# Emitting the first batch's routing at the head of the next quad in a fused attention, top-1 MoE and FFN kernel

## The chip, the core and the metric

The kernel runs on one core of a Trainium2 chip. The metric is the device time of one launch in microseconds. Of the engines, PE (TensorE) does all matmuls and the transposes through the identity, DVE (VectorE) and ACT (ScalarE) empty its PSUM banks and prepare operands, POOL (GpSimd) does elementwise work in SBUF, and SP (SyncE) issues most DMAs. Each engine takes its instructions strictly in the order of the built program, so an instruction that waits holds up all that stand behind it on its engine.

## What is computed

```
q_p, k_p = phi(q_s), phi(k_s)            # random features, exp(h - max) per row; 4 batches, 8 heads, 576 tokens
kv = einsum('bhsm,bhsd->bhmd', k_p, v); z = k_p.sum(2)
attn = einsum('bhsm,bhmd->bhsd', q_p, kv) / (einsum('bhsm,bhm->bhs', q_p, z)[..., None] + 1e-6)
x = attn.transpose(0, 2, 1, 3).reshape(2304, 512)
logits = x @ w_gate                      # 8 experts, each token goes to its argmax
out[mask] = gate_w[mask, None] * (relu(x[mask] @ w1[e]) @ w2[e])
h = out @ w_in; g = h * sigmoid(1.702 * h); y = g @ w_out
```

## The kernel before

The attention works on **quads** of four heads, two quads to a batch, eight in all. For quad `i`, `kgen(i)` projects the keys (`ph_P`, PSUM tile `pr`) and sums `kv_ps`; `qgen(i)` runs 17 steps on the queries in the order `Q_ORDER`: `P` projects (`pr`, L350 and L351), `X` transposes (`tq`, L430), `N` forms the normalised output (`num`, L444), `R` transposes it for the MoE (`tx`, `small`, L464 and L466). Each `P` takes a row maximum and a subtraction on DVE (L359, L368, L380). `halves_T` splits the next quads' inputs into two f16 halves (ACT L307, POOL L308, squares on POOL L267 and L272) and sends them through a transposing DMA on SP (`xT`, L309, three buffers).

When both quads of a batch are done, `route(b)` finds the expert that most of the batch's tokens chose: logits on PE (`lT_ps`, L529 and L530), transposes (`lg_ps`, L537), a chain of small DVE operations (L542 to L554, `oh` is the one-hot), a count over all partitions on PE (`ct_ps`, L561), and its argmax on DVE (`es`, L571). SP loads `es` into a register (L604), and with it issues the loads of that expert's weights (`st`, L674, eight chunks of 512 KB for a batch). ACT and POOL (DVE for the first chunk and for the last batch) split each chunk into `wh` and `wl` (L698, L700). `moe_gen(b)` then multiplies in three passes (L136; PSUM tiles `m_ps` and `w_ps`), 384 matmuls of 128x288 for a batch, with `h1h` on ACT (L732) and `h1l` on DVE (L735) between its two layers. Tokens that chose another expert than their batch's are counted and would be done by a general loop behind it.

The order of the program has three sources. The generators of attention are merged by weight: `merge` always advances the generator that has the smallest share of steps done over weight. The main loop runs attention alone until the first batch's gate stands (`while 0 not in gate_t`), then alternates attention and MoE by accumulated cost, counted from the point at which MoE began. And a scheduler reorders instructions by priority when the program is built. `route` has seven steps; the weights are 17 for `qgen`, `ROUTE_N` = 10 for `route` and 5 for `kgen`. From tick 245 of the loop on, jobs for the FFN's weights (`prep_outs`, `z` tiles on DVE, `raw_o` loads and `wo_dram` stores issued by ACT) are mixed in. The FFN follows when the MoE is done.

## Time and profile before

| | us |
|---|---|
| median of 3 runs | 768.23 (766.17 to 768.77) |
| the profiled execution: time | 767.65 |
| its span, first to last instruction | 765.6 |
| PE busy in the span | 739.7 (97%) |
| DVE, ACT, POOL busy | 531.3, 338.6, 131.9 |
| mean granted TensorE clock | 0.99 of full speed |

PE is busy nearly all of the span, so a microsecond is lost or won where PE waits or runs at a lower clock. The share of the span says little by itself; the stretches in which PE is not full are few, and they are what to read.

### The profile page before, as it was taken

What the parts mean: (1) busy time and instruction counts of PE and PEld (TensorE: products, weight loads), DVE (VectorE), ACT (ScalarE), POOL (GpSimd) and SP (SyncE); (2) the same over time, 40 slices, a digit from 0 to 9 for tenths busy, and PEclk for the clock granted to TensorE, in tenths of its full rate; (3) what the DMA queues carried; (4) which work ended last, traced back from release to release, by engine and by line L of the source; (5) the groups of instructions that cost most, each with busy time, mean ns of one, the idle gap of its engine ahead of it and who ended that gap; (6) DMA issues with size and microseconds to landing.
All of it is one profiled execution on the core that took longest, in us unless ns stands there. A gap on an engine that the chain in (4) does not pass through costs nothing.

```text
span 765.6 us, 14359 instructions
## 1 busy us (share of the span) xinstructions
PE 739.7 (97%) x5559; PEld 716.1 (94%) x5559; DVE 531.3 (69%) x1188; ACT 338.6 (44%) x638; POOL 131.9 (17%) x78
## 2 busy tenths in 40 slices
PE   7998799999999999989999999999999999999997
PEld 6877699999999999979999999999999999999996
DVE  5867867586776685556879559981368777777774
ACT  5554464335522332233427464554576433444331
POOL 3563377609500441000000000000000000000000
PEclk9999799999999999999999999999999999999999
DMA  5447594456725554198145558972978544443311
GB/s 157 117 131 187 123 302 97 120 140 193 189 60 162 150 179 134 51 234 287 59 161 197 177 171 295 316 263 100 332 273 298 172 138 138 137 129 117 115 29 32
DMA packets 136715, 127.57 MB, mean 167 GB/s; under 512 B 58176, under 2 KB 120896, under 8 KB 135744
## 3 DMA queue, kind: packets, MB, share of 16 engines
q1 hardware_dynamic: 123936, 98.85, 43.5%
q10 hardware_dynamic: 12704, 27.73, 10.3%
q8 instruction: 45, 0.74, 0.4%
q14 instruction: 30, 0.25, 0.1%
HBM read 79.68 MB, written 40.40 MB: 157 GB/s over the span
## 4 chain that ended last, share of the span: by engine, by line
PE 83%; DVE 8%; DMA 4%; issue 1%; ACT 1%; SPq 1%; POOL 0%; ACTq 0%; POOLq 0%; DVEq 0%
PE m_ps L136 19%; PE qa L1249 13%; PE qa L1146 13%; PE qm L1249 7%; PE w_ps L136 4%; PE pb L1249 3%; PE qm L1146 3%; PE qu L1146 3%; PE num L444 3%; PE kv_ps L402 3%; DMA st<-in_moe_w_dram 2%; PE qn L1146 2%; PE qt L1146 2%; PE tq L430 1%; PE pr L344 1%
## 5 line engine op out<-in xcount | busy, mean ns | idle before, releaser
L1146 PE MATMUL qa<-y,wi 128*128 128x384 f32 x576 | 109.2, 337 | 0.4 <-DVE g L901 0.4
L1146 PEld LDWEIGHTS qa<-y,wi 128*128 128x128 f32 x576 | 101.4, 188 | 0.8 <-DVE g L901 0.8
L136 PE MATMUL m_ps<-xh,wh 128*128 128x288 f32 x256 | 79.0, 309 | 4.1 <-DVE h1l L735 2.3
L136 PE MATMUL m_ps<-xh,wl 128*128 128x288 f32 x256 | 76.8, 300 | 0.1
L136 PE MATMUL m_ps<-xl,wh 128*128 128x288 f32 x256 | 76.4, 298 | 0.0
L700 POOL TENSOR_TENSOR wl<-st,wh 128x1024 fp32r<-128x1024 f32 x23 | 55.1, 2401 | 83.0 <-ACT wh L698 82.9
L359 DVE TENSOR_REDUCE small<-pr 128x4 f32<-128x512 f32 (+1 forms) x80 | 51.1, 639 | 11.8 <-PE pr L351 7.8
L698 ACT ACTIVATE wh<-st 128x1024 fp32r<-128x1024 f32 (+1 forms) x33 | 34.0, 1035 | 48.5 <-DMA st<-in_moe_w_dram 31.6
L136 PEld LDWEIGHTS m_ps<-xh,wh 128*128 128x128 f32 x256 | 48.6, 190 | 5.8 <-DVE h1l L735 3.6
L136 PE MATMUL m_ps<-h1h,wh 128*128 128x288 f32 x160 | 48.8, 305 | 0.9 <-DVE h1l L735 0.9
L136 PEld LDWEIGHTS m_ps<-xh,wl 128*128 128x128 f32 x256 | 48.6, 190 | 0.5 <-DVE wl L700 0.4
L735 DVE SCALAR_TENSOR_TENSOR h1l<-m_ps,h1h 128x288 fp32r<-128x288 f32 x64 | 28.9, 453 | 28.9 <-ACT h1h L732 28.8
L136 PEld LDWEIGHTS m_ps<-xl,wh 128*128 128x128 f32 x256 | 48.6, 190 | 0.0
L136 PE MATMUL m_ps<-h1l,wh 128*128 128x288 f32 x160 | 47.7, 298 | 0.0
L136 PE MATMUL m_ps<-h1h,wl 128*128 128x288 f32 x160 | 47.4, 298 | 0.0
L732 ACT ACTIVATE h1h<-m_ps 128x288 fp32r<-128x288 f32 x64 | 25.9, 407 | 48.5 <-PE m_ps L136 46.7
L1249 PE MATMUL qa<-p,p 128*128 128x256 f32 x360 | 46.2, 282 | 1.1 <-DVE p L855 0.8
L1249 PE MATMUL qa<-p,gs 128*128 128x256 f32 x360 | 45.9, 282 | 0.0
L1249 PEld LDWEIGHTS qa<-p,p 128*128 128x128 f32 x360 | 44.2, 189 | 1.6 <-DVE p L855 1.0
L1249 PEld LDWEIGHTS qa<-p,gs 128*128 128x128 f32 x360 | 44.2, 189 | 0.0
L444 PEld LDWEIGHTS num<-kv,qpT 128*128 128x128 f32 (+1 forms) x320 | 36.7, 184 | 5.4 <-ACT qpT L432 3.1
L444 PE MATMUL num<-kv,qpT 128*128 128x65 f32 (+1 forms) x320 | 39.3, 266 | 2.5 <-ACT qpT L432 1.4
(213 smaller groups left out, 1819.5 us busy)
## 6 DMA issues: line engine op xcount, KB each, us to landing
g_dram<-g ACTq DMA_DIRECT2D x48, 384.0 KB, 4.1
st<-in_moe_w_dram SPq DMA_DIRECT2D x31, 512.0 KB, 5.2
pg<-g_dram SPq DMA_DIRECT2D x10, 1024.0 KB, 5.7
raw<-in_moe_w_in_dram SPq DMA_DIRECT2D x16, 512.0 KB, 4.0
gt<-g_dram SPq DMA_DIRECT2D x8, 1024.0 KB, 5.4
p<-wo_dram SPq DMA_DIRECT2D x6, 1024.0 KB, 7.3
yt<-y_dram SPq DMA_DIRECT2D x12, 384.0 KB, 6.0
vm<-in_v_dram SPq DMA_DIRECT2D x32, 128.0 KB, 3.2
```

Source lines behind the costliest of these rows:

```text
L136: ins = nc.tensor.matmul(out=ps, lhsT=a, rhs=b, start=start and n == 0, stop=stop and n == 2)
L344: nc.tensor.matmul(out=ps[:, :, h2], lhsT=xT[:, (2 * pr + h2) * 2 + t0 // 2], rhs=wbd)
L359: nc.vector.tensor_reduce(out=pm, in_=ps[:, :w], axis=AX.X, op=ALU.max, negate=on_act)
L402: nc.tensor.matmul(out=kv_ps[:, h, :], lhsT=kp[j // 2][:, j % 2, h2, :], rhs=vm[:, h, t, :], start=(t == 0), stop=False,)
L430: nc.tensor.transpose(tq[:, c, h2], qp[i][:, c, h2, :], ident)
L444: nc.tensor.matmul(out=ps[:n, c, h2, :], lhsT=lhsT, rhs=kv[:, h, :])
L698: nc.scalar.activation(out=hi[:, :, s], in_=st[:, :, s], func=ACTF.Copy)
L700: eng.tensor_tensor(out=lo[:, :, s], in0=st[:, :, s], in1=f32(hi)[:, :, s], op=ALU.subtract)
L732: nc.scalar.activation(out=hh[:, f], in_=ps, func=ACTF.Relu)
L735: nc.vector.scalar_tensor_tensor(out=hl[:, f], in0=ps, scalar=0.0, in1=f32(hh[:, f]), op0=ALU.max, op1=ALU.subtract)
L1146: ins = nc.tensor.matmul(out=ps, lhsT=w[:, a, ks], rhs=y[:, b, kk], start=start and kk + m == 0, stop=kk == 1 and m == 2, skip_group_check ...
L1249: ins = nc.tensor.matmul(out=ps, lhsT=x[:, f], rhs=w[i][:, f], start=start and f + m == 0, stop=f == NP - 1 and m == 2, skip_group_check=True,
```

## The change

The weight of `route` among the three generators is 40 in place of 10 for the first batch, whose routing is merged with `qgen(2)` and `kgen(3)`; for the other batches it stays 10. `pending` is the batch's number, so it is zero for the first batch alone.

```
             if pending is not None:
-                parts.append((route(pending), ROUTE_N))
+                parts.append((route(pending), ROUTE_N if pending else 40))
                 pending = None
```

With weight 10 the seven steps of the routing stand at shares of 0 to 0.6 of the quad; with 40 at 0 to 0.15, so all of them lie within the first three steps of `qgen(2)`. The gate of the first batch then stands earlier in the program, and with it the point from which MoE is mixed in.

On SP, before, the two transposing DMAs of the fifth quad's inputs stand ahead of the register load of `es` and of the weight loads (ISA rows set registers):

```order
L258 DMA m<-in_q_dram 64x2x64
L309 DMA_TRANSPOSE xT<-hl 128x18x128 x2
L604 TENSOR_LOAD es
L674 ISA
L674 DMA st<-in_moe_w_dram 128x4x128
L674 ISA
L674 DMA st<-in_moe_w_dram 128x4x128
```

Now the register load follows the last input load directly, and the two transposing DMAs stand behind all nine weight issues:

```order
L258 DMA m<-in_q_dram 64x2x64
L604 TENSOR_LOAD es
L674 ISA
...
L674 DMA st<-in_moe_w_dram 128x2x512
L612 DMA r_dram<-rr 64x2
L309 DMA_TRANSPOSE xT<-hl 128x18x128
L504 DMA x_dram<-xn 64x256
L309 DMA_TRANSPOSE xT<-hl 128x18x128
```

On PE, before, the count over the first batch's tokens stands between two projections, 40 rows behind the transposes `lg_ps` of its logits:

```order
L351 LDWEIGHTS xT
L351 MATMUL pr<-wl_118,xT 128x128
L561 MATMUL ct_ps<-oh,ones 128x40
L350 LDWEIGHTS xT
L350 MATMUL pr<-wh_117,xT 128x128
```

Now it stands next to them, with one step `X` between, and all later projections, up to the first `m_ps`, stand behind it:

```order
L351 MATMUL pr<-wl_118,xT 128x128
L537 MATMUL lg_ps<-ident,lT 128x16 x2
L537 MATMUL lg_ps<-ident,lT 64x16
L430 MATMUL tq<-ident,qp 128x128 x4
L561 MATMUL ct_ps<-oh,ones 128x40
L350 LDWEIGHTS xT
L350 MATMUL pr<-wh_117,xT 128x128
```

Between the last `lT_ps` and the first `m_ps` of the first batch, PE before has 64 `pr` matmuls, 18 `tq`, four `num` steps, one `R` step's transposes and the routing's own; now it has 40 `pr`, 14 `tq` and one `num` step. The rest stands behind the first `m_ps`.

On DVE at the fourth batch's routing, before, the register value `es` stands two rows behind an `h1l`, and two further `h1l` of the third batch stand between it and the second weight split `wl` of the fourth:

```order
L735 SCALAR_TENSOR_TENSOR h1l<-m_ps,h1h 128x288
L835 SCALAR_TENSOR_TENSOR z<-raw_o,z 128x512
L571 CAST es<-ci 128x1
...
L1046 CAST tot_i<-small 128x1
L700 TENSOR_TENSOR wl_4355<-st,wh_4354 128x1024
L735 SCALAR_TENSOR_TENSOR h1l<-m_ps,h1h 128x288 x2
L700 TENSOR_TENSOR wl_4394<-st,wh_4393 128x1024
```

Now two `h1l` stand between `es` and the first `wl`, and one `h1l` between the first `wl` and the second:

```order
L571 CAST es<-ci 128x1
...
L735 SCALAR_TENSOR_TENSOR h1l<-m_ps,h1h 128x288
L831 SCALAR_TENSOR_TENSOR z<-raw_o,z 128x512
L735 SCALAR_TENSOR_TENSOR h1l<-m_ps,h1h 128x288
...
L1046 CAST tot_i<-small 128x1
L831 SCALAR_TENSOR_TENSOR z<-raw_o,z 128x512
L700 TENSOR_TENSOR wl_4351<-st,wh_4350 128x1024
```

Counted in MoE matmuls of L136 that stand ahead of them on PE, the counts `ct_ps` of the second, third and fourth batch stand behind 276, 555 and 987 before, and behind 317, 591 and 964 now; the batches begin at 384, 768 and 1152.

## Rows read from the trace of the kernel before

**Rows 1.** Windows: start and end, length, busy time of each engine, clock, DMA
```profile
73.50:94.25 20.75, 14.63 (x127) 12.40 (x126) 17.06 (x82) 9.04 (x25) 8.41 (x5) 0.84 0.41 92
94.25:97.60 3.35, 3.17 (x13) 2.73 (x13) 2.79 (x7) 3.31 (x9) 0.00 (x0) 0.55 1.05 356
100.00:280.00 180.00, 180.00 (x1586) 173.47 (x1585) 125.38 (x394) 73.27 (x138) 80.93 (x39) 1.00 0.55 154
324.00:356.00 32.00, 28.47 (x202) 26.78 (x201) 19.28 (x38) 12.38 (x20) 0.00 (x0) 1.00 0.86 240
```

**Rows 2.** Chain that ended last, PE at full clock: start, us on the chain
```profile
98.20 0.06 PE pr L350
...
152.28 0.44 PE tq L430 x4
152.72 0.84 PE num L444 x8
...
169.52 0.61 PE num L444 x8
...
174.65 0.44 PE tx L464 x4
...
374.41 3.20 PE m_ps L136 x24
```

**Rows 3.** SP's DMA queue in order of time, 72 to 97.5 us: start, us
```profile
82.01 5.73 SPq L309 DMA_TRANSPOSE xT<-hl  x2
89.22 5.97 SPq L674 DMA_DIRECT2D st<-in_moe_w_dram  x8
```

**Rows 4.** In order of time: first batch's count, register value, first MoE matmul
```profile
85.77 0.16 DVE L565 TENSOR_REDUCE ct<-ct_ps 128x8 f32<-128x40 f32 x1
...
88.26 0.15 DVE L571 CAST es<-ci 128x1 int32<-128x1 uint32 x1
...
94.30 0.40 PE L136 MATMUL m_ps<-xh,wh 128*128 128x288 f32 x1 [1.73 <-ACT wh L698]
```

**Rows 5.** ACT, POOL and DVE in order of time around the first routing
```profile
73.41 0.69 ACT L531 ACTIVATE lT<-lT_ps 16x288 f32<-16x288 f32 x2 [2.42 <-PE lT_ps L530]
...
74.72 1.40 POOL L272 TENSOR_TENSOR m<-m 128x576 f32<-128x576 f32 x1
76.63 2.38 POOL L308 TENSOR_TENSOR hl<-m,hl 128x1152 f16<-128x1152 f32 x1 [0.52 <-DVE small L359]
79.08 2.11 POOL L267 TENSOR_TENSOR m<-m 128x1152 f32<-128x1152 f32 x1
...
79.58 0.21 DVE L542 COPY lg<-lg_ps 128x64 f32<-128x64 f32 x1
...
79.90 1.35 DVE L545 TENSOR_TENSOR lg<-lg 128x40 f32<-128x40 f32 x1
...
83.46 0.07 DVE L552 MEMSET oh<- 64x8 f32 x1
```

**Rows 6.** The same operation at the third batch's routing, POOL idle: DVE in time
```profile
231.63 0.20 DVE L545 TENSOR_TENSOR lg<-lg 128x40 f32<-128x40 f32 x1
```

**Rows 7.** Who waited for whom, PE, 320 to 360 us: total, times, longest
```profile
PE m_ps L136 <- DVE h1l L735: 3.0, 4, 0.9
PE w_ps L136 <- ACT h1h L732: 0.6, 1, 0.6
```

**Rows 8.** DVE in order of time, 336 us
```profile
336.45 0.43 DVE L826 TENSOR_SCALAR z<-raw_o 128x512 int32<-128x512 int32 x1 [2.72 <-DMA raw_o<-in_moe_w_out_dram]
```

**Rows 9.** In order of time: second batch's count and its first weight split
```profile
165.88 0.37 PE L561 MATMUL ct_ps<-oh,ones 128*128 128x40 f32 x2
...
177.80 2.37 POOL L700 TENSOR_TENSOR wl<-st,wh 128x1024 fp32r<-128x1024 f32 x1
```

**Rows 10.** Window of m_ps alone, from that count to the second batch's first matmul
```profile
165.88:193.42 27.54, 16.32 (x107) 14.60 (x108) 2.25 (x5) 0.41 (x1) 1.00 0.76 219
```

**Rows 11.** What SP's DMA queue waited for, 55 to 110 us: total, times, longest
```profile
SPq L309 <- PE pr L351: 11.3, 2, 9.4
```

## Prediction

> **What bounds the kernel now.** I read the windows first, to find where PE is not full. From 100 to 280 us PE is busy 180.00 of 180.00 us at a granted clock of 1.00 [rows 1]: there the time is PE's own work, and a reordering that adds and removes nothing wins nothing. Two stretches are different. From 73.5 to 94.25 us PE is busy 14.63 of 20.75 us, at a mean clock of 0.84, while DVE is busy 17.06: attention runs alone, as a chain of short steps from PE to DVE or ACT and back, and the first batch's routing lies within it. From 324 to 356 us PE is busy 28.47 of 32.00 us, 3.53 us short [rows 1]; the list of waits puts 3.0 us of it on `h1l` (DVE, L735) and 0.6 on `h1h` [rows 7]. This is the place where the fourth batch's weights arrive late: DVE splits them itself and holds `h1l` back behind a split or behind a job that waits. One such job, `z`, waited 2.72 us for its own load [rows 8].
>
> The first stretch ends with a wait that reaches back to the routing. `es` is ready at 88.26 + 0.15 = 88.41 us, and the first MoE matmul starts at 94.30, after 1.73 us of waiting for the split `wh` [rows 4]. So from `es` to the first MoE matmul it takes 5.89 us: register load, transfer, first split. SP had been held by two transposing DMAs at 82.01 to 87.74 [rows 3]; that is shortly before `es`, so `es` and not SP set the time.
>
> **The change part by part.** It removes and adds no work. It moves the routing's steps ahead on PE and DVE, the weight loads ahead of two transposing DMAs on SP, and, since MoE begins earlier in the program, a part of the second batch's attention from before the first MoE matmul to behind it.
>
> *What the move costs on PE.* By the counts in the section on the change, 24 `pr` matmuls, 4 `tq`, 3 `num` steps and one `tx` step leave the stretch in which PE waits anyway, and go into the stretch in which it is full. At full clock they take 24 x 0.06 = 1.44, 0.44, 0.84 + 0.84 + 0.61 = 2.29 and 0.44 us on the chain [rows 2]: 4.6 us. Before, these 4.6 us were free, since they lay beside the wait for `es` and the weights. So the first MoE matmul has to start 4.6 us earlier, at 89.7 in place of 94.30, for the move to come out even. Each microsecond later is a microsecond lost, each one earlier is won.
>
> *When it will start.* Up to the logits nothing changes: `lT` is copied at 73.41 to 74.10 [rows 5]. PE then does the transposes `lg_ps`, and DVE's copy can start near 74.9 in place of 79.58. From that copy to the cleared one-hot `oh` it took 83.53 - 79.58 = 3.95 us, in which L545 took 1.35 us [rows 5]; the same operation took 0.20 us at the third batch's routing, where POOL was idle [rows 6]. Here POOL's L267 ran from 79.08 to 81.19, and L545 ended at 81.25 [rows 5]: I read this as DVE waiting for POOL's instruction to end. Without that wait the piece is 2.8 us, and `oh` would be ready at 77.7. But the earlier place puts the chain beside more of POOL's work: L272 (74.72 to 76.12), then L308 (2.38 us), then L267 (2.11 us) [rows 5], which come back to back there. L545 would reach DVE near 75.2 and wait some 0.7 us more. The next operations of its kind are L551 and L554 (two inputs in SBUF). If each meets POOL's next instruction, they wait 1.0 us (L308, now from about 76.15 to 78.5) and 2.0 us (L267). So `oh` is ready at 78.4, 79.4 or 81.4, by one, two or three such waits.
>
> The Trainium skill, SBUF — State Buffer, section "SBUF: two separate sides", says that a DVE operation with two SBUF inputs and a POOL instruction that reads SBUF exclude each other for the whole instruction. By that rule all three wait, and the start would come out at the late end; by the row of L545 alone, the only one that shows it, at the early end. The change would then win 2.2 us at the start in place of losing 0.8 (worked out below).
>
> From `oh` on: the count now stands next on PE, which waits for it with nothing else to do. It takes 0.37 us [rows 9], some 0.6 with the way back, and from L565 to the end of `es` it was 88.41 - 85.77 = 2.64 us [rows 4]. That makes `es` ready 3.2 us after `oh`, at 81.6, 82.6 or 84.6, and the first MoE matmul, 5.89 us later, at 87.5, 88.5 or 90.5. Against 89.7 this is a gain of 2.2, a gain of 1.2 or a loss of 0.8 us. I take the last: in the trace DVE and POOL take turns (POOL's next instruction started at 81.27, right behind L545), so an operation that has just waited lets POOL's next one in ahead of the following. If further small operations are caught as well, one more turn of 2.11 us gives a loss of 2.9. Below nothing the bound is the 2.2 us.
>
> *What must be done by then.* Six projections stand between the count and the first MoE matmul, now behind a PE that waited 4 to 6 us for `oh`. Before, PE went from the first `pr` of this group to the last in some 7.4 us, with the count's operations on DVE among them, so they should be done by about 87.5 to 89.7, within a microsecond of the weights. If that cover is gone, PE waits for them instead of the weights, one to one. The clock stays as it is: the first twelve MoE matmuls run at a mean clock of 0.55 from 94.25 to 97.60 [rows 1], and I expect the same behind the new wait.
>
> *What else stands behind SP's weight loads.* The two transposing DMAs (5.73 us of SP's queue [rows 3]) now follow nine issues, of which eight took 5.97 us. They are issued near 95 in place of 82, and the fifth quad needs them behind 72 MoE matmuls (9.6 us at 3.20/24 each [rows 2]) and some 6 us of attention, near 108. They lie beside that work and cost nothing; were they later than that, PE would wait one to one.
>
> *The fourth batch.* The order of the loop shifts all later routings: the fourth count stands behind 964 MoE matmuls in place of 987. That is 23 x 0.133 = 3.1 us earlier [rows 2], against the same need. Of the five waits, I expect the first two (1.2 us, the first splits) and the one behind the waiting `z` (0.6 us) to go, since the splits now stand before one `h1l` fewer and the load has 3.1 us more. The other two stay. Gain 1.8 us, between 0 and 3.5.
>
> *Sum.* +0.8 - 1.8 = -1.0 us. Against the profiled execution's own 767.65 us that is 766.65. It lies 0.6 us below the median of 768.23, from which it would be 767.2; I predict 767.0. That is within 0.3% (2.3 us), about what a measurement of this kernel can tell from no change.
>
> **The rivals.**
>
> *Both ends gain.* POOL catches L545 alone or DVE gets the turn, so MoE starts at 87.5, and the fourth batch's waits all go: -2.2 - 3.5 gives 762.5 from the median, and half of this, 765.4, is already faster by over 0.3%. For it: SP is free from 72.5 us on, and nothing but `es` holds the loads. Against it: the pattern of turns above. 0.32.
>
> *The second batch's weights come late (slower).* Its count stands behind 317 MoE matmuls in place of 276, with its need still at 384. From the count at 165.88 to the first `wl` at 180.17 it took 14.3 us [rows 9], and the 108 `m_ps` up to the second batch took 27.54 us [rows 10], so 13.3 us were to spare. Forty-one matmuls at 27.54/108 = 0.255 us are 10.5 us, and 2.8 us are left. It decides if this chain takes 2.8 us longer than before. A transposing DMA that SP holds for a free `xT` buffer stands ahead of this `es` too, and one such wait was 9.4 us [rows 11]: 9.4 - 2.8 = 6.6 us of PE, 773.8. Half of it gives 770.5. 0.12.
>
> *The weights are not earlier.* The DVE operations are traced earlier but run no earlier, since POOL and the in-order queue hold them, and `es` stays near 88.4. Then the 4.6 us of moved attention are lost whole: 768.23 + 4.6 - 1.8 = 771.0. For it: DVE is busy 17.06 of 20.75 us there [rows 1]. Against it: PE alone held `lg_ps` and the count back by some 4 us before. 0.10.
>
> **How the numbers follow.** The forecast, a start from even to 1.5 us worse and an end 1 to 3 us better, has 0.46, with a range of its own from 765.9 to 768.7. With the rivals, faster by over 0.3% is 0.32, within 0.46, slower 0.12 + 0.10 = 0.22. The range from 764.2 to 771.0 leaves out the far half of the first rival and of the second.
>
> **What would show it.** In the changed profile: L545 over 0.5 us and L551 or L554 over 1 us beside POOL's instructions; PE's `ct_ps` with an idle time of 3 us or more before it; `es` near 84.6; the first `m_ps` near 90.5, after a wait for `wh`; fewer `pr`, `tq` and `num` ahead of it; PE full from some 95 us to 280; the idle time of PE in its fourth batch under 2.5 us. The prediction is wrong if the first `m_ps` starts before 88.5 or after 92.6, if PE has idle time at the second batch's start, or if the fourth batch's waits are as long as before.

## The result, and the profile after

The changed kernel takes 773.21 us (median of 9 runs, 770.17 to 777.03) where the kernel before takes 768.77 (9 runs, 765.72 to 774.00): a ratio of 1.006 (1.0031 to 1.0089), 0.6% slower. The forecast was 767.0, in a range of 764.2 to 771.0, and was wrong. The profiled execution took 770.25 us, its span is 768.2.

Executions differ ahead of the change already: `lT`, the last instruction that the change leaves alone, was copied at 73.41 us before [rows 5] and at 71.68 now, and in the executions told of below between 70.3 and 74.8. So times below are counted from `lT` where two kernels are compared.

**The start.** After, ACT, POOL, DVE, PE and SP in order of time around the first routing (start, us):

```profile
71.68 0.69 ACT L531 ACTIVATE lT<-lT_ps 16x288 f32<-16x288 f32 x2 [2.42 <-PE lT_ps L530]
...
72.99 1.40 POOL L272 TENSOR_TENSOR m<-m 128x576 f32<-128x576 f32 x1
73.38 1.07 DVE L545 TENSOR_TENSOR lg<-lg 128x40 f32<-128x40 f32 x1
74.49 2.36 POOL L308 TENSOR_TENSOR hl<-m,hl 128x1152 f16<-128x1152 f32 x1
75.34 1.57 DVE L551 TENSOR_TENSOR oh<-lg,rm 128x40 f32<-128x40 f32 x1
76.83 0.19 DVE L554 TENSOR_TENSOR ex<-lg,rm 128x40 f32<-128x40 f32 x1
76.93 2.11 POOL L267 TENSOR_TENSOR m<-m 128x1152 f32<-128x1152 f32 x1
77.65 0.07 DVE L552 MEMSET oh<- 64x8 f32 x1
77.87 0.62 PE L561 MATMUL ct_ps<-oh,ones 128*128 128x40 f32 x2 [4.27 <-DVE oh L552]
78.23 0.83 DVE L591 CAST ixf<-lix 128x5 f32<-128x5 uint32 x1
81.66 0.14 DVE L571 CAST es<-ci 128x1 int32<-128x1 uint32 x1
82.53 5.46 SPq L674 DMA_DIRECT2D st<-in_moe_w_dram  x8
85.83 0.40 PE L136 MATMUL m_ps<-xh,wh 128*128 128x288 f32 x1 [0.17 <-ACT wh L698]
...
90.93 6.91 SPq L309 DMA_TRANSPOSE xT<-hl  x1
```

L545 is held to the end of POOL's L272 (74.39 us) and L551 to the end of L308 (76.85): two turns. L554 fits into the 0.08 us between L308 and L267 and pays nothing. Behind `oh` a third operation is held: the cast L591, to the end of L267 (79.04), and DVE's reading of the count (L565) stands behind it, at 79.91. PE's count waits 4.27 us for `oh`. The first `m_ps` starts 14.15 us after `lT`; before it was 94.30 - 73.41 = 20.89 [rows 4, 5].

**The stretch that was full.** After, windows (start and end, length, busy time of PE, PE's weight loads, DVE, ACT and POOL, granted clock, DMA share, GB/s):

```profile
73.50:94.25 20.75, 15.05 (x126) 13.77 (x126) 17.69 (x77) 10.90 (x25) 10.48 (x6) 0.84 0.52 170
85.80:89.20 3.40, 2.88 (x21) 2.75 (x22) 2.27 (x6) 0.63 (x1) 0.00 (x0) 1.00 0.99 307
100.00:280.00 180.00, 174.47 (x1516) 166.82 (x1516) 121.63 (x389) 67.85 (x131) 71.25 (x34) 0.97 0.58 147
180.00:200.00 20.00, 16.33 (x131) 15.43 (x130) 11.15 (x34) 8.83 (x15) 15.30 (x8) 0.83 0.74 180
190.00:195.00 5.00, 3.00 (x18) 2.52 (x18) 4.76 (x12) 3.30 (x7) 5.00 (x4) 0.50 0.49 111
250.00:280.00 30.00, 28.47 (x214) 27.57 (x214) 21.02 (x43) 9.95 (x19) 10.07 (x4) 0.94 0.81 244
324.00:356.00 32.00, 29.62 (x215) 28.40 (x214) 20.02 (x44) 12.62 (x20) 0.00 (x0) 1.00 0.73 214
```

The row that was 180.00 busy at a clock of 1.00 [rows 1] is 174.47 at 0.97 now. Of its 5.53 idle us, 3.67 lie in 180 to 200 us and 1.53 in 250 to 280; in 190 to 195 the granted clock is 0.50 besides. The fourth batch's window is idle for 2.38 us where it was 3.53.

**How the stall at 190 us comes about.** After, SP, ACT, DVE and PE in order of time at the second batch's weights (in brackets the engine's idle time before the row, and who ended it):

```profile
173.03 0.99 SPq L674 DMA_DIRECT2D st<-in_moe_w_dram  x2
...
175.85 2.15 SPq L790 DMA_DIRECT2D y_dram<-y  x4
179.37 3.36 SPq L258 DMA_DIRECT2D m<-in_q_dram  x2
182.97 1.94 SPq L674 DMA_DIRECT2D st<-in_moe_w_dram  x2
187.02 1.16 ACT L307 ACTIVATE hl<-m 128x1152 f16<-128x1152 f32 x1 [6.46 <-DMA st<-in_moe_w_dram]
188.09 0.21 ACT L469 ACTIVATE xh<-small 128x64 fp32r<-128x64 f32 x1
188.33 0.22 DVE L473 TENSOR_TENSOR xl<-small,xh 128x64 fp32r<-128x64 f32 x1 [6.77 <-ACT xh L469]
190.70 0.26 PE L350 MATMUL pr<-wh,xT 128*128 128x128 f16 x1 [2.37 <-DVE qp L380]
192.27 1.11 PE L430 MATMUL tq<-ident,qp 128*128 128x128 f32 x4 [1.30 <-DVE xl L473]
```

Read it from the end. PE waits for what stands on DVE behind the `xl` at 188.33; that `xl` waited 6.77 us for ACT's `xh`, a copy of 0.21 us, and `xh` stands behind ACT's L307, before which ACT idled 6.46 us. L307 splits the last quad's queries. (Its bracket names an `st`, but the profile lists L307 with 6.5 us as the one that waited for the loads L258.) Their last two loads (L258, 32 KB each) were issued by SP at 179.37, behind two `st` and four `y` stores, and took 3.36 us of SP's queue; the second pair of `st` follows at 182.97. What held the two loads stands in the list of what SP's queue waited for (after, 160 to 195 us: total, times, longest):

```profile
SPq L258 <- DMA r_dram<-rr: 3.3, 2, 2.0
```

They waited on SP for the landing of the two stores of the routing's result (`r_dram`, L609 and L612, issued at 174.12 and 174.62, landed 5.2 and 7.4 us later); in the trace each of the loads signals its landing by the same semaphore as the store that it waited for. So two jobs for later work, the last quad's `hl` and the second batch's next `wh`, make ACT wait for a DMA, and everything that PE's attention needs from ACT waits behind them. MoE matmuls, which would fill PE's gap, have run ahead: 396 of L136 lie ahead of 184 us, and the next, at 193.46, stands on PE behind the attention steps that wait (in e10 below, where they don't, it starts at 189.28, ahead of the third split). Before there were 364 by 184 us, and 19 more by 193.3.

**An account of lost PE time.** To compare kernels in which matmuls stand in another order, I summed from PE's rows, for each matmul, the time to the next one's start less that form's usual interval (the median: 0.133 us for `m_ps` and `w_ps`, 0.056 for `pr`, 0.109 for `tq` and `tx`, 0.112 for `num` and `kv_ps`). It holds idle time and low clock alike. The columns are stretches in us after `lT`; "count" is the number of MoE matmuls ahead of the fourth batch's `ct_ps`; "rest" is the span less `lT`. The table covers one profiled execution of each kernel, and those lie up to some 5 us from the medians of many runs at its right.

| kernel | 0-30 | 30-110 | 110-130 | 130-250 | 250-300 | sum | rest | count | median, before beside it | ratio (95%) |
|---|---|---|---|---|---|---|---|---|---|---|
| before | 12.6 | 1.2 | 0.3 | 2.9 | 5.5 | 22.6 | 692.2 | 987 | | |
| after | 10.0 | 1.9 | 5.9 | 5.6 | 3.7 | 27.1 | 696.5 | 964 | 773.21, 768.77 | 1.0060 (1.0031-1.0089) |
| e1 | 10.1 | 2.7 | 3.2 | 2.2 | 7.6 | 25.7 | 695.0 | 984 | 769.10, 767.57 | 1.0027 (1.0007-1.0047) |
| e2 | 13.2 | 1.3 | 1.7 | 3.1 | 5.0 | 24.3 | 693.6 | 987 | 768.74, 767.57 | 1.0010 (0.9993-1.0028) |
| e3 | 10.4 | 6.4 | 2.1 | 5.5 | 4.1 | 28.5 | 698.1 | 964 | 770.29, 767.57 | 1.0031 (1.0002-1.0060) |
| e4 | 13.6 | 1.7 | 5.2 | 2.1 | 5.0 | 27.7 | 697.0 | 975 | 770.94, 767.57 | 1.0038 (1.0011-1.0066) |
| e5 | 10.2 | 2.6 | 6.1 | 4.1 | 4.0 | 27.0 | 696.4 | 964 | 772.70, 767.69 | 1.0067 (1.0042-1.0091) |
| e6 | 9.9 | 1.3 | 5.7 | 2.3 | 3.7 | 22.9 | 692.4 | 954 | 768.05, 767.69 | 0.9995 (0.9979-1.0012) |
| e7 | 10.5 | 2.8 | 6.6 | 3.2 | 12.4 | 35.6 | 705.5 | 955 | 778.10, 767.69 | 1.0132 (1.0118-1.0147) |
| e8 | 13.1 | 1.6 | 3.4 | 3.2 | 7.6 | 28.9 | 698.4 | 984 | 769.69, 767.69 | 1.0030 (1.0016-1.0045) |
| e9 | 9.8 | 1.3 | 4.9 | 6.6 | 2.6 | 25.2 | 694.5 | 954 | 770.16, 767.43 | 1.0035 (1.0010-1.0059) |
| e10 | 10.7 | 2.8 | 0.4 | 5.9 | 6.6 | 26.5 | 695.7 | 984 | 769.00, 767.43 | 1.0018 (0.9994-1.0041) |
| e11 | 14.5 | 1.2 | 0.2 | 3.1 | 6.7 | 25.8 | 695.2 | 987 | 767.86, 767.43 | 0.9995 (0.9980-1.0011) |
| e12 | 9.1 | 1.4 | 6.3 | 2.9 | 1.9 | 21.6 | 691.1 | 954 | 765.37, 767.84 | 0.9981 (0.9952-1.0011) |
| e13 | 9.2 | 2.0 | 1.1 | 4.5 | 8.5 | 25.2 | 694.7 | 984 | 766.43, 767.72 | 0.9985 (0.9958-1.0011) |
| e14 | 10.6 | 2.9 | 0.9 | 2.9 | 5.2 | 22.5 | 691.9 | 987 | 768.54, 767.72 | 1.0007 (0.9984-1.0030) |
| e15 | 9.1 | 3.0 | 1.7 | 3.6 | 3.4 | 20.8 | 690.4 | 956 | 762.59, 766.78 | 0.9925 (0.9907-0.9944) |
| e16 | 7.6 | 1.2 | 1.3 | 6.5 | 5.3 | 21.7 | 691.3 | 954 | 767.75, 766.78 | 1.0012 (0.9992-1.0031) |

From before to after: -2.6 at the start, +0.7, +5.6 at the second batch, +2.7 behind it, -1.8 at the fourth batch: 4.5 us more lost, as the rest of the span grew by 4.3 and the medians by 4.4. So both ends came out as a gain, and more than they gave was lost between them.

### The profile page after: what moved, and what is told of

It reads as the page before. It is cut to its first block, busy times and chain, and to the rows that moved or that the text cites. A ratio compares the mean times of both kernels' runs of the same rounds, so it can differ in the third digit from the quotient of the medians.

```text
span 768.2 us, 14369 instructions
## 1 busy us (share of the span) xinstructions
PE 738.9 (96%) x5559; PEld 716.3 (93%) x5559; DVE 530.7 (69%) x1188; ACT 337.4 (44%) x638; POOL 132.9 (17%) x78
## 3 DMA queue, kind: packets, MB, share of 16 engines
q10 hardware_dynamic: 12704, 27.73, 10.7%
## 4 chain that ended last, share of the span: by engine, by line
PE 78%; DMA 8%; DVE 6%; ACT 2%; POOL 2%; issue 1%; SPq 1%; ACTq 0%; POOLq 0%; DVEq 0%
PE m_ps L136 16%; PE qa L1249 13%; PE qa L1146 13%; PE qm L1249 7%; DMA st<-in_moe_w_dram 5%; PE w_ps L136 4%; PE pb L1249 3%; PE qm L1146 3%; PE qu L1146 3%; PE num L444 3%; DMA m<-in_k_dram 2%; PE pr L344 2%; PE qn L1146 2%; PE tq L430 2%; PE qt L1146 2%
## 5 line engine op out<-in xcount | busy, mean ns | idle before, releaser
L136 PE MATMUL m_ps<-xh,wh 128*128 128x288 f32 x256 | 79.1, 309 | 2.6 <-DVE h1l L735 1.8
L136 PE MATMUL m_ps<-xl,wh 128*128 128x288 f32 x256 | 76.3, 298 | 0.0
L136 PE MATMUL m_ps<-xh,wl 128*128 128x288 f32 x256 | 75.9, 297 | 0.0
L359 DVE TENSOR_REDUCE small<-pr 128x4 f32<-128x512 f32 (+1 forms) x80 | 51.0, 638 | 12.4 <-PE pr L351 9.3
L698 ACT ACTIVATE wh<-st 128x1024 fp32r<-128x1024 f32 (+1 forms) x33 | 34.1, 1033 | 47.6 <-DMA st<-in_moe_w_dram 35.7
L136 PEld LDWEIGHTS m_ps<-xh,wh 128*128 128x128 f32 x256 | 48.5, 189 | 4.4 <-DVE h1l L735 2.8
L136 PE MATMUL m_ps<-h1h,wh 128*128 128x288 f32 x160 | 49.9, 312 | 0.4 <-DVE h1l L735 0.4
L136 PE MATMUL m_ps<-h1h,wl 128*128 128x288 f32 x160 | 48.4, 302 | 0.3 <-POOL wl L700 0.3
L136 PEld LDWEIGHTS m_ps<-xl,wh 128*128 128x128 f32 x256 | 48.4, 189 | 0.1
L136 PEld LDWEIGHTS m_ps<-xh,wl 128*128 128x128 f32 x256 | 48.3, 189 | 0.1
L136 PE MATMUL m_ps<-h1l,wh 128*128 128x288 f32 x160 | 48.2, 302 | 0.0
L732 ACT ACTIVATE h1h<-m_ps 128x288 fp32r<-128x288 f32 x64 | 25.7, 405 | 50.2 <-PE m_ps L136 49.4
L432 ACT ACTIVATE qpT<-tq 128x512 f32<-128x512 f32 (+1 forms) x40 | 22.1, 551 | 43.8 <-PE tq L430 36.9
```

The costliest lines, as they stand in the source:

```text
L136: ins = nc.tensor.matmul(out=ps, lhsT=a, rhs=b, start=start and n == 0, stop=stop and n == 2)
L359: nc.vector.tensor_reduce(out=pm, in_=ps[:, :w], axis=AX.X, op=ALU.max, negate=on_act)
L432: nc.scalar.activation(out=qt[i][:, :w], in_=tq[:, :w], func=ACTF.Exp)
L698: nc.scalar.activation(out=hi[:, :, s], in_=st[:, :, s], func=ACTF.Copy)
L732: nc.scalar.activation(out=hh[:, f], in_=ps, func=ACTF.Relu)
```

## The experiments

Four theories were set against each other. **A**: loads at the second batch's start come late behind other transfers on SP (at first the last quad's query loads alone, later whichever load ACT waits for), and ACT's queue, waiting for them in order, starves PE; another order there takes the loss away. **B**: PE is merely ahead of those loads, having done the first batch's matmuls sooner; the loss then stands in any order, or moves on to the next late thing. **C**: the time is lost at the start, or by accidents of the order elsewhere, and not in this wait. **D**: the second batch's routing lags in the program, and a weight of 40 for it too is the cure.

### The load, the routing's weight, and the mirror

**e1**: the last quad's query loads go to SP ahead of what stands there.

```
-            load_qk(q, q_in, i + 1)
+            with tc.high_priority() if i == 6 else nullcontext(): load_qk(q, q_in, i + 1)
```

> The change, with the two remainder transfers (L258) of the last quad's queries put directly behind their main transfer on SP, ahead of the second batch's routing, weights and y stores. Theory A (a late load): in the changed kernel ACT's split L307 of these queries waits 6.46 us at 187.02, because the remainders are issued only at 179.37, and holds xh, DVE's xl and PE behind it. Then ACT's wait shrinks below 2 us, PE is busy over 19 of 20 us from 180 to 200 at a clock above 0.95, and the time is 4 to 6 us under the changed kernel, some 0.4% faster than the kernel before. Theory B (the second batch is bound by its data): PE is merely ahead there, and the wait goes to the next late thing, kp, st or wl, so PE still lacks 3 us or more between 180 and 210, and the time stays within 1.5 us of the changed kernel. Theory C (the start lost it): the time stays slower than the kernel before even with PE full from 180 to 200.

The loss at the second batch falls from 5.9 to 3.2 us and comes in waits of 1.39 us at most; the clock of 180 to 200 us is 1.00 with PE busy 17.39. The time falls to 1.0027, where A had it 0.4% under the kernel before. The late loss rose (3.7 to 7.6), so not all that was won is seen in the time. A has the place right; half of the loss stays, though, as B would have it: now the four `y` stores hold SP's queue, for 6.04 us at 177.53, and `st` follows at 183.91.

**e2**: the mirror, in the kernel before. The last two query loads have to follow an `x_dram` store; the one meant was issued at 180.69 in the kernel before.

```
-            ), after)
+            ), kept[-1] if dst is q_in and i == NQ - 1 else after)
...
-            nc.sync.dma_start(
+            kept.append(nc.sync.dma_start(
```

> The kernel before, with the same two remainder transfers put behind the fifth quad's main x_dram store (L501), which was issued at 180.69, in place of 174.33. The mirror of the run above: nothing of the routing moves. Theory A: ACT's L307 of the last quad's queries starts near 186 in place of 179.79, PE loses 3 to 4 us between 186 and 196 and half of its clock for a while, and the time is 3 to 6 us over the kernel before, as much as the change. Theory B: the second batch has slack here that the changed kernel lacked, PE loses under 1 us, and the time is the same. Theory C expects no change either.

1.4 us more are lost there (0.3 to 1.7), and the time stays (1.0010). It is no mirror. The loads came to stand behind a later store (SP's queue in e2):

```profile
211.77 1.62 SPq L258 DMA_DIRECT2D m<-in_q_dram  x2
```

Before, they were issued at 174.33. ACT's L307 went with them, to 215.0, so nothing of it waits between 180 and 200 us. The run tests neither half of A: the 3 to 6 us that A expected aren't there, but neither is the wait that was to cause them.

**e3**: 40 for the second batch's routing too.

```
-                parts.append((route(pending), ROUTE_N if pending else 40))
+                parts.append((route(pending), 40 if pending < 2 else ROUTE_N))
```

> The change, with four times the share for the second batch's routing too, so that its count stands behind 276 matmuls m_ps again, as in the kernel before, in place of 317. Theory A: what decides is only whether the remainders of the last quad's queries are issued before or behind the routing's load of the expert's number and its weights; the routing is earlier here, so unless they stand ahead of it, ACT's L307 still waits over 4 us and PE lacks 2 us or more between 175 and 200. The time is 768 to 773. Rival D (the relative lateness of the second batch's routing): with its count back at 276 the stall goes, PE is full from 180 to 200, and the time is 764 to 766.

D fails. The weights come sooner, and ACT waits for them sooner. ACT in order of time:

```profile
177.87 1.06 ACT L698 ACTIVATE wh<-st 128x1024 fp32r<-128x1024 f32 x1 [4.70 <-DMA st<-in_moe_w_dram]
178.83 0.58 ACT L432 ACTIVATE qpT<-tq 128x512 f32<-128x512 f32 x1
```

Now a `wh` split waits 4.70 us for its `st`, and `qpT` is held behind it; PE waits 2.1 us for that. The loss moved to an earlier stretch (30-110: 6.4).

**e4**: a smaller weight, 20.

```
-                parts.append((route(pending), ROUTE_N if pending else 40))
+                parts.append((route(pending), ROUTE_N if pending else 20))
```

> The first batch's routing at weight 20, half of the change: its count stands behind 89 matmuls pr (73 with the change, 109 before), the first m_ps behind 125 (109 and 133), the second count behind 307 m_ps (317 and 276). Theory A: the start gains about half, 1 to 2 us, and the stall in the second batch is there or not, by the place of the remainders in SP's queue, all or nothing. Rival D (it grows with the lag of the second routing): three quarters of the stall, 4 us. Theory C (the start loses): half of the loss, 2 us over the kernel before, with PE full from 180 to 200.

The second batch's loss is nearly that of 40 (5.2), and the start's gain is gone (13.6; `m_ps` waits 3.1 us for `wh`). The weight is no dial between the two kernels.

### ACT's order

**e5**: L307 of the last quad stands behind the next instruction of ACT's program order (`behind(x, n)` fixes that an instruction comes after the last n ahead of it on its engine).

```
-            nc.scalar.activation(out=hl[:, c, 0], in_=m[:, c], func=ACTF.Copy)
+            behind(nc.scalar.activation(out=hl[:, c, 0], in_=m[:, c], func=ACTF.Copy), 1 if src is q_in and i == NQ - 1 else 0)
```

> The change, with ACT's split L307 of the last quad's queries held behind the ACT work traced before it (its x copies among them); no transfer is moved. In the changed kernel that split waited 6.46 us for its data with the copy xh behind it. Theory A (ACT's order: what waits for a landing holds the next attention step): xh at 188.09 comes 4 us or more earlier, PE's waits at 190.70 and 192.27 (2.37 and 1.30 us) go, PE keeps its clock from 180 to 200, and of the 5.6 us lost there at least 4 come back: 768 to 769.5. Theory B (PE is merely ahead of its data and waits for the next late thing): PE still lacks 2.5 us or more between 180 and 200, and the time is within 1.5 us of the changed kernel. A risk to both: the split is now so late that the last quad's projections wait for it, which would show as PE waiting for xT after 220.

772.7 us, the changed kernel's time (1.0067). ACT and PE in order of time:

```profile
189.17 1.06 ACT L698 ACTIVATE wh<-st 128x1024 fp32r<-128x1024 f32 x1 [7.09 <-DMA st<-in_moe_w_dram]
190.43 0.59 ACT L469 ACTIVATE xh<-tx 128x512 fp32r<-128x512 f32 x1
191.79 1.12 PE L430 MATMUL tq<-ident,qp 128*128 128x128 f32 x4 [3.04 <-DVE xl L473]
```

With L307 out of the way the third `wh` split waits 7.09 us in the same place, with `xh` behind it, and PE idles 3.04 us in one piece. That is what B expected. So A in its first form, that ACT's wait for the small query loads is the whole of it, falls. Two ACT jobs wait for DMAs there, and taking one away shows the other.

**e6**: the second batch's splits are held back as well.

```
-                nc.scalar.activation(out=hi[:, :, s], in_=st[:, :, s], func=ACTF.Copy)
+                behind(nc.scalar.activation(out=hi[:, :, s], in_=st[:, :, s], func=ACTF.Copy), 4 if b == 1 else 0)
```

> As the run above, and each split L698 of the second batch's weights is held behind the four ACT operations traced before it too, so that fewer attention copies stand behind a wait for a landing. Theory A: nothing on ACT with a wait of over 2 us for a transfer has xh or qpT of attention directly behind it between 175 and 200, and PE is as full there as in the kernel before (20 of 20 us, clock 1.00): 766.5 to 768.5, unless the weights now come late for the second batch's matmuls, which would show as PE waiting for wh or wl. Theory B: PE still lacks 2.5 us or more.

The time is that of before (0.9995), but not for the expected reason: the third split still waits (7.12 us), the loss there is 5.7. What fell is the loss behind it (5.6 to 2.3): PE's 250 to 280 us are 29.86 busy at a clock of 1.00.

**e7**: e5, and the FFN's weight jobs begin at tick 252.

```
-    OUT_FROM = 245
+    OUT_FROM = 252
```

> As e5_hl_behind, and the jobs that decode the expert-free layer's output weights on DVE (z, L826 to L901) begin seven steps of the loop later. In the changed kernel one of them (L831) took 2.30 us at 264.76, while POOL's wl ran from 264.13 to 266.51, in place of 0.67, and xl of attention stood behind it; PE lost 3.8 us from 262 to 282, half of it by its clock. If that is the cause of the second loss, PE is busy over 29.5 of 30 us from 250 to 280 at a clock of 1.00 here, and the time is 2 to 4 us under e5_hl_behind. If the loss comes with the order in general, it turns up at another place within 30 us and the time is that of e5_hl_behind within 1.5 us.

From 250 to 280 us PE is busy 29.49 us, where it was 28.68 in e5, so those jobs take part in the loss there; but moved behind, they cost the fourth batch 12.4 us (with one wait for `h1l` of 5.3), and the time is 778.1.

**e8**: a weight of 30.

```
-                parts.append((route(pending), ROUTE_N if pending else 40))
+                parts.append((route(pending), ROUTE_N if pending else 30))
```

> The first batch's routing at weight 30 in place of 40. What stands on PE ahead of the first count and ahead of the first m_ps is the same as with 40 (73 and 109 pr), and the second count stands behind 315 m_ps in place of 317: the start is the same, and what follows is ordered a little otherwise. Theory A or B (a loss that belongs to the early start): PE lacks 3 us or more between 175 and 200 here too, and the time is within 2 us of the changed kernel, 771 to 774. Theory C (an accident of one order): the start gains the same 2.5 us, the stall is not there or at half its size, and the time is 766 to 769.

The start was to be that of 40, and isn't (13.1): L551 took 2.06 us, and the first weight tile landed 4.8 us after its issue, where it was 2.6 in the profile after. The second batch's loss is 3.4, the late one 7.6. The profiled execution is the slowest of the twelve (774.24), and the median lies between what C (766 to 769) and what A or B (771 to 774) expected: the run decides nothing.

### The third split

**e9**: e5, and the third split comes later in the program as well.

```
-        while n and prep["split"] < min(prep["free"], prep["staged"]):
+        while n and prep["split"] < min(prep["free"], prep["staged"]) and (prep["split"] != 2 * NW + 2 or clock[0] > 165):
...
+                behind(nc.scalar.activation(out=hi[:, :, s], in_=st[:, :, s], func=ACTF.Copy), 4 if b == 1 and c == 2 else 0)
```

> As e5_hl_behind, and the third split L698 of the second batch's weights is traced two steps of the loop later and held behind the ACT work traced before it, so that it stands behind the copy xh of the fifth quad. In e5_hl_behind that split waited 7.09 us for its tile st (issued at 184.2, behind the remainders of the last quad's queries and behind wl, which frees the buffer), with h1h and xh behind it in ACT's order; DVE's xl and PE's tq waited for xh (3.0 us). Theory A, as it now stands (second batch's loads come late against attention's copies that ACT's order puts behind them, whichever load it is): PE's wait for xl goes, PE is busy over 19 of 20 us from 180 to 200 with its clock at 1.00, and 3.5 us or more of e5's time come back: 768 to 769.5. Theory B (PE has simply run out of filling work, and the attention chain is too short of it): the wait moves on to qp or kp, and PE still lacks over 2 us between 183 and 197.

ACT and PE in order of time:

```profile
184.34 0.59 ACT L469 ACTIVATE xh<-tx 128x512 fp32r<-128x512 f32 x1
191.56 1.06 ACT L698 ACTIVATE wh<-st 128x1024 fp32r<-128x1024 f32 x1 [6.63 <-DMA st<-in_moe_w_dram]
192.52 0.61 ACT L386 ACTIVATE kp<-kp 128x512 f32<-128x512 f32 x1
194.25 0.59 ACT L432 ACTIVATE qpT<-tq 128x512 f32<-128x512 f32 x1
194.89 0.66 PE L430 MATMUL tq<-ident,qp 128*128 128x128 f32 x4 [2.34 <-ACT qpT L432]
```

`xh` starts at 184.34, and the split, waiting 6.63 us, holds `kp` and `qpT` in its place: one victim goes, the next is found. PE is busy 17.16 of 20 us and the time 770.16, as B expected, and not A's 768 to 769.5; what PE waits for is, as A has it, again a copy behind a split.

**e10**: e6 and that condition of the third split.

```
+        while n and prep["split"] < min(prep["free"], prep["staged"]) and (prep["split"] != 2 * NW + 2 or clock[0] > 165):
...
+                behind(nc.scalar.activation(out=hi[:, :, s], in_=st[:, :, s], func=ACTF.Copy), 4 if b == 1 else 0)
```

> As e6_acts_behind, with the third split moved likewise. e6_acts_behind was at the kernel before's time although PE lost 5.6 us between 180 and 200 to that one wait (2.74 us and the half clock behind it). Theory A: this comes back, less what the order costs elsewhere: 763 to 766, under both kernels by 0.3% or more. Theory B: no change against e6, 767 to 769. If the order behind it turns out worse (the losses from 250 to 360 us moved by 2 to 4 us from one run to the next), 766 to 768.

ACT in order of time, and the window:

```profile
184.57 0.59 ACT L469 ACTIVATE xh<-tx 128x512 fp32r<-128x512 f32 x1
...
188.84 0.39 ACT L410 ACTIVATE kv<-kv_ps 128x260 f32<-128x260 f32 x1 [0.73 <-PE kv_ps L406]
190.16 1.06 ACT L698 ACTIVATE wh<-st 128x1024 fp32r<-128x1024 f32 x1 [0.93 <-DMA st<-in_moe_w_dram]
```

```profile
180.00:200.00 20.00, 20.00 (x189) 19.46 (x188) 16.15 (x46) 9.83 (x20) 9.16 (x4) 1.00 0.85 195
```

With `xh`, `kp` and `kv` ahead of the waiting split, PE is busy 20.00 of 20.00 us at 1.00, and 0.4 us are lost where it was 5.9, though the MoE matmuls have run ahead as far (396 by 184 us in both). For the stall this decides between A and B: it is the order of ACT's queue, and PE's being ahead doesn't force it. For the time it doesn't: 1.0018 (0.9994 to 1.0041) is no less than e6 with its stall (0.9995), as B expected (767 to 769) and not A (763 to 766); 5.9 and 6.6 us are lost in the last two stretches.

**e11**: the two holds of e6 (L307 of the last quad, L698 of the second batch) in the kernel before.

> The kernel before with the two holds of e6_acts_behind and the routing where it was. It tells whether e6_acts_behind owes its time to the early routing plus the holds, or to the holds alone. In the kernel before PE waited for nothing between 180 and 200, so by theory A the holds have nothing to give there: within 1.5 us of the kernel before, 766.5 to 769. If the holds help by themselves (fewer steps of ACT behind a landing everywhere in the second batch), 764 to 766.

No gain (0.9995): the holds are worth nothing where the stall isn't.

### The start, and a version that beats both

**e12**: e6, with the split of the fifth quad's queries held back on ACT too, so that POOL's turn after it moves.

```
-            behind(nc.scalar.activation(out=hl[:, c, 0], in_=m[:, c], func=ACTF.Copy), 1 if src is q_in and i == NQ - 1 else 0)
+            behind(nc.scalar.activation(out=hl[:, c, 0], in_=m[:, c], func=ACTF.Copy), 1 if src is q_in and i in (4, NQ - 1) else 0)
```

> As e6_acts_behind, and ACT's split L307 of the fifth quad's queries is held behind the ACT work traced before it, so that POOL's L308 and L267, which need its result, leave the place beside the first batch's routing. In the changed kernel L551 took 1.57 us there, beside POOL's L308 (74.49 to 76.85), and L545 took 1.07 us beside POOL's L272 (72.99 to 74.39), in place of 0.20. If DVE's operations with two inputs in SBUF wait there for POOL's instruction to end, L551 takes 0.2 us, the cleared one-hot oh, es and the first m_ps come 1.3 to 1.4 us earlier after the copy lT, and PE loses 8.6 us in the 30 us from lT in place of 9.9: the time is 1.3 us under e6_acts_behind, if the later order is as good, 766 to 768. If POOL is not what makes L551 long, it stays near 1.5 us and the first m_ps where it was. L545 stays near 1 us by both, since L272 is not moved.

In order of time around the first routing:

```profile
70.61 0.69 ACT L531 ACTIVATE lT<-lT_ps 16x288 f32<-16x288 f32 x2 [2.44 <-PE lT_ps L530]
71.89 1.40 POOL L272 TENSOR_TENSOR m<-m 128x576 f32<-128x576 f32 x1
72.32 1.03 DVE L545 TENSOR_TENSOR lg<-lg 128x40 f32<-128x40 f32 x1
74.24 0.18 DVE L551 TENSOR_TENSOR oh<-lg,rm 128x40 f32<-128x40 f32 x1
78.43 0.15 DVE L571 CAST es<-ci 128x1 int32<-128x1 uint32 x1
82.68 0.40 PE L136 MATMUL m_ps<-xh,wh 128*128 128x288 f32 x1 [0.44 <-ACT wh L698]
```

L551 takes 0.18 us with POOL idle, L545 still 1.03 beside L272, and `es` comes 7.82 us after `lT`, the first `m_ps` 12.07 after it, in place of 9.98 and 14.15. L551 gives 1.39 us of that, and the cast L591, which takes 0.16 us here in place of 0.83, gives 0.67. PE loses only 0.8 us less there than in e6 (9.1 for 9.9), and the time (0.9981) lies within the intervals of e6.

**e13**: e10 and e12 together.

> The change with all holds: e10_acts_split_late (no wait of PE from 180 to 200) and e12_pool_turn (a start 1 to 2 us better) in one. If the start and the second batch's stall are two separate terms, both show here: PE has lost about 9 us by 30 us after lT and under 13 by 130 us after it, against 14.1 in the kernel before and 17.8 in the changed one, and the time is 762 to 765, unless the order from 250 to 360 us loses 3 us more again, as in e10_acts_split_late (then 765 to 768). If what is won comes back as a later loss by itself (PE, being ahead, waits for the next late thing), the time is that of e12_pool_turn, 765 to 766, at best.

1.1 us are lost at the second batch, 8.5 at the end; 0.9985 (0.9958 to 1.0011), which isn't told from no change.

**e14**: the same holds as e12's (L307 of the fifth and the last quad, L698) in the kernel before.

> The kernel before with the holds of e12_pool_turn and its routing at the old weight: what the holds give without the change. POOL's L308 and L267 are then away from the first batch's routing here too; in the kernel before L545 took 1.35 us beside L267 (79.08 to 81.19), so it should take 0.2, and es comes up to 1.1 us earlier, but PE still has 101 matmuls pr ahead of the first count, in place of 81 in e12_pool_turn. If the early routing is worth something beyond the holds, this is 1.5 us or more over e12_pool_turn: 766 to 768. If the holds do it all, 764 to 766.

L545 takes 0.20 us as with an idle POOL, and the time stays (1.0007): the holds alone give nothing that these runs can tell.

**e15**: e13, and 7 for the third batch's routing, which brings the fourth's count forward from behind 984 matmuls to 956.

```
-                parts.append((route(pending), ROUTE_N if pending else 40))
+                parts.append((route(pending), (40, 10, 7)[pending]))
```

> As e13_pool_turn_split, with the third batch's routing at weight 7 in place of 10, which puts the fourth batch's count behind 888 matmuls m_ps and 68 w_ps in place of 912 and 72; up to the third batch nothing stands otherwise. Over the kernels run so far, those with the fourth count behind 888 to 892 m_ps lost 1.9 to 3.9 us of PE between 250 and 300 us after lT, those with 912 lost 5.0 to 8.4, e13 itself 8.4. If the fourth count's place makes the difference (the prediction's fourth batch term), PE loses under 4 us there, and with e13's 16.7 us up to 250 it has lost under 21 at 300, against 22.6 in the kernel before: 761 to 764, faster than the kernel before by 0.4% or more. If those losses are accidents of the order, 764 to 767 as e13.

762.59 us (6 runs) against 766.78 for the kernel before: 0.9925 (0.9907 to 0.9944). Window:

```profile
180.00:200.00 20.00, 18.62 (x155) 17.90 (x155) 15.40 (x43) 10.16 (x19) 9.44 (x4) 0.91 0.68 177
```

It keeps the start (9.1), loses 1.7 at the second batch and 3.4 late. It beats both kernels. Beside e12, which has the same start (9.1) and nearly the same count (954), it has lost less at the second batch (1.7 for 6.3), and its interval lies below e12's (0.9952 to 1.0011): that is the nearest that the runs come to what the stall costs in the whole time. How much the third batch's weight gives alone isn't separated: the weight of 7 wasn't tried in the kernel before.

**e16**: e13 with another way to the early count, the pace of attention against MoE in the main loop.

```
-    A_RATIO = 1.15
+    A_RATIO = 1.13
```

> As e13_pool_turn_split, with the ratio of attention to expert steps in the loop at 1.13 in place of 1.15, a second way to the same place: the fourth count stands behind 888 m_ps and 66 w_ps, the second behind 316, the third behind 600. The whole order from the first batch on is another, so that a stall may appear at any place up to 250 us. If the fourth count's place decides the late loss, PE loses under 4 us between 250 and 300 us after lT here too, whatever it lost before.

The count is as early (954), and the time is 1.0012 (0.9992 to 1.0031): 6.5 us are lost behind the second batch and 5.3 late, where less than 4 was expected. An early fourth count alone doesn't make the gain, and neither does an early count with the stall cured (1.3 at the second batch).

## Why the prediction was wrong

**The step that failed** is the first reading: "from 100 to 280 us ... a reordering that adds and removes nothing wins nothing". It was taken as if it could lose nothing either, and the middle entered the sum as 0. By the account the runs show some +8 there (5.6 at the second batch, 2.7 behind it). For the first the cause is shown: it goes when ACT's order changes (e10, e13). That the whole time comes down with it isn't shown, since e6 keeps it (5.7) and is as fast as the kernel before, and e10 without it is no faster. The second stays open (below). Two of the prediction's own signs of being wrong came: PE idled at the second batch's start, and the first `m_ps` lay ahead of 88.5 (at 85.83, or 87.56 with the `lT` of before). That PE is full says how well the order of before covers each wait, and not how much cover is left.

**The slower rival** had the place and the lateness right (second batch's loads late against a need that moved up, 0.12, 770.5 to 773.8), and its consumer wrong. I took the slack, 2.8 us, against `m_ps`, the reader of `wh` and `wl`. What ran out was ACT's: its splits are issued in order ahead of copies that attention needs at once, so the need was earlier than the first `m_ps`. The step of a transposing DMA that waits for a buffer played no part; the late loads were two of 32 KB that waited 3.3 us on SP for two stores, and the `st` behind them. That the measured time lies in this rival's range is in part luck.

**The cost of the move and its break-even**, 16.3 us from `lT` to the first `m_ps`, fits: the start came 2.1 us below it, and the account gives 2.6 won.

**The time of the start** had the wrong sign in the sum (+0.8, with -2.2 as the lower bound). `oh` was cleared 5.97 us after `lT`, which is the value for two turns (6.0); I had chosen three (8.0). L545 and L551 waited, and L554, taken as the third, slipped in ahead of POOL's L267. By the rule of the Trainium skill, SBUF — State Buffer, section "SBUF: two separate sides", an operation of DVE with two SBUF inputs and a POOL instruction that reads SBUF exclude each other, and the one that starts first keeps the ports for its whole length; the trace agrees for the two that met one (1.07 and 1.57 us, where 0.20 and 0.18 stand with POOL idle). The rule doesn't say which of two that wait is next, and that decided here. `es` was ready 10.12 us after `lT` (two turns: 9.2); the turn of L591, which the prediction had as a risk only, is 0.67 of the difference. From `es` to `m_ps` it took 4.03 us, not 5.89 [rows 4]; the first weight tile landed 2.6 us after SP's issue, in other executions up to 4.8. Why isn't shown.

**The projections and the clock.** The projections were done in time. The clock behind the wait was to stay low; the first `m_ps` ran at 1.00 (85.80 to 89.20) where it was 0.55 [rows 1], and the half level fell on the small matmuls of attention ahead of them. How much of the gain that is, isn't separated.

**The transposing DMAs** were issued at 90.93 and 98.57 (not near 95) and cost nothing in this profile; in seven of the experiments PE waits 0.6 to 1.2 us for `xT`.

**The fourth batch** was right in size: 1.8 us predicted, 1.8 by the account, 1.15 by the window. Two waits for `h1l` of 1.8 us in all are left of four with 3.0, and one for `h1h` of 0.5. But the longest is one behind a `z` job that waits for a DMA, of the kind that was to go (after, DVE and PE in order of time):

```profile
329.36 0.43 DVE L826 TENSOR_SCALAR z<-raw_o 128x512 int32<-128x512 int32 x1 [3.23 <-DMA wo_dram<-z]
...
330.26 0.40 PE L136 MATMUL m_ps<-xh,wh 128*128 128x288 f32 x1 [1.12 <-DVE h1l L735]
```

So the size is in part luck. Over the experiments, a count behind 954 to 964 goes with a late loss of 1.9 to 5.3 us (e7 apart, in which other jobs were moved there), and one behind 975 to 987 with 5.0 to 8.5; e16 shows that the two touch.

**Left open** is the loss at 260 to 280 us (after, POOL, DVE and PE in order of time):

```profile
264.13 2.38 POOL L700 TENSOR_TENSOR wl<-st,wh 128x1024 fp32r<-128x1024 f32 x1 [3.56 <-ACT wh L698]
264.76 2.30 DVE L831 SCALAR_TENSOR_TENSOR z<-raw_o,z 128x512 int32<-128x512 int32 x1
269.62 0.65 PE L464 MATMUL tx<-ident,xn 128*128 128x128 f32 x4 [1.14 <-DVE xl L473]
```

A `z` job of 0.68 us elsewhere takes 2.30 beside POOL's `wl`, DVE's `xl` comes late, PE waits. That alone isn't the cause: the kernel before has the like, beside a `wl` at 260.10, and PE is full there (before, DVE):

```profile
260.73 2.28 DVE L831 SCALAR_TENSOR_TENSOR z<-raw_o,z 128x512 int32<-128x512 int32 x1
```

From 250 to 280 us PE is busy 30.00 of 30.00 in e1, e4, e8 and the three variants of the kernel before (e2, e11, e14), 29.2 to 29.9 in e6, e7, e12 and e15, 28.3 to 28.7 in e3, e5, e9, e10 and e13, and 27.8 in e16. That goes with neither the weight of 40 nor the count alone, and no edit was found that takes it away and leaves the rest. And one profile for each kernel tells places, not the last microsecond: e13's sum is above that of before, its median is 1.3 us below.

## What to carry to other kernels

Where a window shows PE full, look for the smallest margin in it before a change that shifts what fills PE: for each load, ask which in-order queue holds an instruction that waits for it, and what stands behind that instruction, since the need of those is the load's due time and not its first direct reader's. When a filler (here the first batch's matmuls) moves ahead, list every place at which it covered a wait before, its end above all. And of several stalls cured one by one, measure the whole time at each step: here the cured place (e10, 0.4 us lost in place of 5.9) brought the time no lower than the kernel before, and only the kernel with start, middle and end in order (e15) beat it.

## What the runs showed of the hardware

- DVE operations with two SBUF inputs took 1.07 and 1.57 us (after), 2.06 (e8) and 2.30 (the `z` job L831) beside a POOL instruction of 1.4 to 2.4 us, and 0.18 to 0.20 (the `z` job 0.68) without; one took 0.19 in a gap of 0.08 us between two POOL instructions. Two with one SBUF input were held as well: the cast L591 took 0.83 us beside L267 and 0.16 without (e12), and L826 1.98 us beside a `wl` (at 258.86) and 0.41 without (at 267.35).
- In and behind a wait of PE's of 2.4 us the granted clock was 0.50, the lower of its two levels (190 to 195 us); 250 to 280 us, with a longest wait of 1.14 us, had 0.94; 180 to 200 us of e1, with waits of 1.39 us and less and 2.6 idle us in all, had 1.00. So the length of the longest wait doesn't tell whether the clock falls.
- Two loads of 32 KB (L258) took 3.36 us of SP's queue at 179.37, where the same pair for the keys took 1.29 at 164.71. The first two waited 3.3 us there for the landing of two earlier stores, whose semaphores they share; the keys' pair waited for none.
